# Fifteen small loads between the fifth K load and the fourth V load of a decode kernel

## The chip, the cores and the metric

The kernel runs on one core of one Trainium2 chip. The metric is device time in microseconds (us), the median of the runs shown. A profile is one execution of the same program recorded by the hardware profiler.

## What is computed

For eight sequences with one new position each, the kernel mixes an attention branch and an MLP branch by a gate. The attention has 32 query heads on 16 K/V heads of size 128 and looks at the last W = 2048 of 8192 cached positions. The model width is 576, the MLP width 4608. The inputs and the output are bf16.

```
W = 2048; rep = 2
q = (x @ wq).reshape(B, Sq, 32, 128).transpose(0, 2, 1, 3)
k = repeat(k_cache[:, :, -W:, :], rep, axis=1); v likewise
p = softmax(einsum("bhqd,bhkd->bhqk", q, k) * 128 ** -0.5)
a = einsum("bhqk,bhkd->bhqd", p, v) -> (B, Sq, 4096) @ wo
h = gelu(layernorm(x) @ w1 + b1)
b = h @ w2 + b2
g = sigmoid((x * gate_w).sum(-1))
out = g * a + (1 - g) * b
```

## The kernel before, in words

Nearly all the bytes are the K and V caches. They are read in sixteen units each (NU = 16, four groups of two sequences by four pieces of 512 positions). A unit of K or of V is one load of 4 MiB to all 128 partitions, 32 KB to each. The units share four slots of a large buffer in SBUF, `RAW` (`take_slot`, L606 to L609); a fifth area behind them holds the first part of wo. `load_item` (L613 to L621) takes the next slot and issues the load on SP's queue (L618), which waits until the slot's last readers are through: the transposes of a K unit on DVE (L718) or the P·V products of a V unit on PE (L755 and the loop around L188).

A K unit is transposed on DVE, multiplied with the query on PE (L732, and L175 for the products that keep their weights), its maximum is taken on DVE (L645), the exponential on ACT (L649), and the probabilities are transposed and spread (L668, L674). A V unit is then multiplied with them, and per group the four pieces are weighed together (`group_weights`, L691). The query projection (wq), the layernorm and w1 of the MLP come first; w2 and wo are the last loads, whose products add into one bank of PSUM (`AccGroup`, L570 on; its matmuls are L579). The two halves of the result are copied out on DVE and ACT (L900, L901) and stored by one DMA (L903), behind which SP waits once more (L904).

All loads are issued by SP, in the order of the program, through one queue: each `dma` names the one before it in `after=last_dma[-1:]`. At the start these are wq in two loads (L407, L408), four small ones, namely x with 8 rows of 1,152 bytes (L410), the gate with 1 row (L411), b1 with 4 rows of 2,304 bytes (L412) and b2 with 1 row of 1,152 bytes (L413), then w1 in two loads (L416, L417). After that the list `stream` (L587 to L594) sets the order: K0, K1, V0, K2, V1, K3, V2, K4, V3, K5 and so on, and at the end the parts of w2 and wo.

A DMA's semaphore grows by 16 when it has landed. The load of a slot counts on that slot's own semaphore; the keys stand in `dma_keys` (L376). All buffers lie in one arena, in the order of the `req` calls (L240 to L277), each aligned to 64 bytes and RAW to 512.

The order on each engine is made by a planner at build time (`_Plan.schedule`, L62 on), with a cost for each operation. It picks the operation that can start first by these costs. A DMA takes 0.35 us of its issuing engine (L43, L97). A load of less than 65536 bytes lands after the loads that are under way and a latency, and does not itself take time of the planner's one DMA channel (L98, L99); a larger one moves `dma_free` by its bytes (L101 to L103).

Of the kernel before, what the change touches and what calls it, by code (L numbers as in the profile page):

```python
# [6 lines left out]
BF = mybir.dt.bfloat16  # L7
# [31 lines left out]
class _Plan:  # L39
# [10 lines left out]
    def add(self, eng, fn, deps=(), name=None, cost=0.1, after=(), prio=0):  # L50
        op = _Op(eng, fn, deps, name, cost, after=after, prio=prio)
        op.idx = len(self.all)
        self.all.append(op)
        return op

    def dma(self, eng, fn, semkey, nbytes, deps=(), name=None, after=(), prio=0):
        op = _Op(eng, fn, deps, name, self.DMA_ISSUE, after=after, is_dma=True, dma_sem=semkey, nbytes=nbytes, prio=prio)
        op.idx = len(self.all)
        self.all.append(op)
        return op  # L60
# [134 lines left out]
def build_kernel(nc, A_x, A_k_cache, A_v_cache, A_wq, A_wo, B_x, B_w1, B_b1, B_w2, B_b2, gate_w, out):  # L195
    B, Sq, D = A_x.shape
# [3 lines left out]
    W = min(4096, max(256, Sk // 4))  # L200
# [8 lines left out]
    ND = 4  # L209
# [13 lines left out]
    out2 = out.rearrange("b s d -> (b s) d")  # L223

    with ExitStack() as es:
        R = {}
        aoff = [0]

        def req(name, nelem, dt, align=64):
            sz = 2 if dt == BF else 4  # L230
            o = aoff[0] + ARENA_BASE
            o = (o + align - 1) // align * align - ARENA_BASE
            R[name] = (o, nelem, dt)
            aoff[0] = o + nelem * sz
# [35 lines left out]
        req("X", 128, F32)  # L270
        req("XS", 2 * 128, BF)
        req("oT", WOP * 8, BF)
        req("BD", NK * 64, BF)
        req("P", 2048, BF)
        req("PC", 2048, BF)
# [30 lines left out]
        def view(name, parts=128):  # L306
            o, n, dt = R[name]
            a = arena[0:parts, o // 2: o // 2 + (n * (2 if dt == BF else 4)) // 2]
            if dt == F32:
                a = a.bitcast(F32)  # L310
            return a
# [31 lines left out]
        out_sb = view("out_sb")  # L343
# [18 lines left out]
        def col(i, parts=128):  # L362
# [10 lines left out]
        OC = 64  # L373

        eng_sems = {e: es.enter_context(nc.semaphore("sem_" + e)) for e in ENGS}
        dma_keys = ["x", "g", "b", "b2", "wq", "w1", "out"] + ["s%d" % i for i in range(ND + 1)] + ["t%d" % i for i in range(5)]  # L376
        dma_sems = {k: es.enter_context(nc.semaphore("dma_" + k)) for k in dma_keys}

        P = _Plan()
        add, dma = P.add, P.dma  # L380
# [7 lines left out]
                   deps=[o_idf], name="r8", cost=0.2)  # L388
# [198 lines left out]
        stream, nk = [], 0  # L587
# [8 lines left out]
        last_dma = [d_w1r]  # L596
# [26 lines left out]
        def query(g):  # L623
            qb_done[g] = []
            for a in range(4):
                def fn(e, a=a):
                    dst = bass.AP(arena, offset=32 * a * AST + aoffs("qbd") + 640 * (g % 2) + 32 * a + 16, ap=[[AST, 32], [160, 4], [1, 16]])
                    src = bass.AP(arena, offset=32 * a * AST + aoffs("q4") + 32 * (NB_ * g + a // 2) + 16 * (a % 2), ap=[[AST, 32], [256, 4], [1, 16]])
                    return e.tensor_copy(dst, src)  # L629
                qb_done[g].append(add("pool", fn, deps=o_q4 + [o_qz, qk_unit.get(NT * (g - 1) - 1)], name="qr%d_%d" % (g, a), cost=0.3))  # L630
# [224 lines left out]
        def bias(i):  # L855
            o_bias.append(AccGroup("m2_b", [(ob[:, 0:8], b2_sb), (ob[:, 8:16], b2_sb)], [d_b2, o_obl, o_obh], cost=0.6, after=[o_hp]).op)
# [17 lines left out]

        query(0)
        bias(0)
        for kind, i in stream:
            {"K": k_item, "V": v_item, "W": wo_chunk, "M": m2_chunk, "B": bias}[kind](i)

        seq = []  # L880
        for t in range(NU):
# [13 lines left out]
        fin = []  # L895
        for j, ev in enumerate(("dve", "act")):
# [3 lines left out]
                    return e.tensor_copy(dst, src)  # L900
                return e.activation(out=dst, in_=src, func=ACTF.Copy)  # L901
            fin.append(add(ev, ev_fn, deps=acc_ops, name="fin%d" % j, cost=0.4, prio=9))
        fin = [dma("sp", lambda e: e.dma_start(out2, out_sb[0:8, :]), "out", 8 * D * 2, deps=fin, name="d_out", after=last_dma[-1:])]  # L903
        add("sp", lambda e: e.sem_inc(eng_sems["sp"], 1), deps=fin, name="final_wait", cost=0.05)  # L904

        P.schedule()
# [6 lines left out]
def bass_gated_mix__sliding_block_cached__mixer_channel_mlp__decode_kernel(  # L913
    nc: bass.Bass,
    A_x: bass.AP,
    A_k_cache: bass.AP,
    A_v_cache: bass.AP,
    A_wq: bass.AP,
    A_wo: bass.AP,
    B_x: bass.AP,  # L920
    B_w1: bass.AP,
    B_b1: bass.AP,
    B_w2: bass.AP,
    B_b2: bass.AP,
    gate_w: bass.AP,
    out: bass.AP,
):
    build_kernel(nc, A_x, A_k_cache, A_v_cache, A_wq, A_wo, B_x, B_w1, B_b1, B_w2, B_b2, gate_w, out)
# [28 lines left out]
```

## Time and profile before

| what | value |
|---|---|
| median of 3 runs | 364.61 us (364.4 to 364.72) |
| span of the profiled execution, first to last instruction | 363.0 us |
| median less that span | 1.6 us |
| PE, DVE, ACT busy | 82%, 64%, 46% of the span |
| mean load rate | 426 GB/s, 154.45 MB in all |
| granted clock of PE, mean | 0.958 |

The time of the profiled execution outside its span is not given by itself; what lies around the span is taken as the difference in the third row.

The page gives, for each engine, its busy time and share of the span, and then the span in 40 slices of about 9.1 us with a digit for the busy tenth. "DMA" is the mean busy share of sixteen DMA engines. The load queue is q1 on the page; q8 and q14 fetch instructions through the same sixteen engines. A packet is one piece that one DMA engine moves: 32 KB for a row of a K or V load, 4 bytes for the write of a semaphore. The chain of waits goes back from the last instruction to what released each step. In a table of windows each row has a stretch of time, its length, the busy time of PE, PEld (weight loads), DVE, ACT and POOL in it with instruction counts, the granted clock, the DMA share and the rate of the loads; the last two count each packet wholly in the window in which it starts, so that in a very short window they can exceed what sixteen engines can do.

### The profile page before, as it was taken

To read this page: it belongs to the slowest core of one execution; us is meant where nothing else is said; L and a number is where in the kernel's file an instruction comes from. 1 tells how busy PE (TensorE), PEld (TensorE's weight loads), DVE (VectorE), ACT (ScalarE), POOL (GpSimd) and SP (SyncE) were. 2 spreads that over 40 slices of the span, in tenths; PEclk is the share of its full clock that TensorE was granted. 3 is DMA by queue.
4 is the path that set the end of the run, shared out by engine and by line. 5 is a ranking of instruction groups with operands and counts; after the bars stand their busy time and mean duration, and the time that the engine had idled before them with its cause. 6 is when DMAs were issued, how large, how long until landed. Compare 5 with 4: busy or idle time off the path is not lost.

```text
span 363.0 us, 4821 instructions
## 1 busy us (share of the span) xinstructions
PE 297.9 (82%) x1954; PEld 125.3 (35%) x1423; DVE 231.4 (64%) x166; ACT 168.6 (46%) x130; POOL 22.9 (6%) x52
## 2 busy tenths in 40 slices
PE   0456366999999979998897979997989698999875
PEld 0111000434252615242433417150615152436742
DVE  0452989576666694929385768566675949295720
ACT  1022106656647463663637373838374554656000
POOL 9032030000010000000100000000000000003000
PEclk9976598999999998999999989999999999999999
DMA  8999999999999999999999999999999999999996
GB/s 347 436 437 406 455 412 455 412 455 412 450 415 451 415 451 413 441 426 441 426 441 426 435 430 437 430 437 428 437 430 437 430 435 430 437 430 433 415 430 257
DMA packets 6102, 154.45 MB, mean 426 GB/s; under 512 B 694, under 2 KB 840, under 8 KB 1228
## 3 DMA queue, kind: packets, MB, share of 16 engines
q1 hardware_dynamic: 6092, 154.30, 98.8%
q8 instruction: 8, 0.13, 0.1%
q14 instruction: 2, 0.02, 0.0%
HBM read 154.29 MB, written 0.01 MB: 425 GB/s over the span
## 4 chain that ended last, share of the span: by engine, by line
DMA 56%; DVE 27%; PE 14%; issue 1%; ACT 1%; SPq 0%; POOL 0%
DMA arena<-in_A_k_cache_dram 47%; DVE arena L718 21%; PE ps L175 6%; DMA arena<-in_B_w_dram 6%; DMA arena<-in_A_x_dram 3%; DVE arena L668 2%; PE ps L188 2%; PE ps L755 2%; PE ps L732 2%; DVE arena L645 1%; PE ps L501 0%; PE ps L579 0%; DVE arena L557 0%; DVE arena L521 0%; ACT arena L536 0%
## 5 line engine op out<-in xcount | busy, mean ns | idle before, releaser
L718 DVE STREAM_TRANSPOSE arena<-arena 128x4096 f32<-128x4096 f32 (+1 forms) x34 | 141.7, 4175 | 21.9 <-DMA arena<-in_A_k_cache_dram 21.9
L674 ACT ACTIVATE arena<-arena 32x2048 bf16<-32x2048 bf16 x60 | 114.5, 1908 | 71.4 <-DVE arena L668 42.9
L175 PE MATMUL ps<-arena 128*128 128x512 bf16 (+3 forms) x531 | 136.1, 402 | 0.0
L188 PE MATMUL ps<-arena 128*128 x840 | 109.5, 277 | 7.3 <-issue 1.2
L188 PEld LDWEIGHTS ps<-arena 128*128 x840 | 81.4, 97 | 34.3 <-issue 19.0
L732 PE MATMUL ps<-arena 128*128 128x512 bf16 x128 | 51.4, 401 | 27.6 <-DVE arena L718 26.1
L645 DVE TENSOR_REDUCE arena<-ps 128x1 f32<-128x2048 f32 x16 | 36.7, 2291 | 53.8 <-PE ps L175 53.8
L732 PEld LDWEIGHTS ps<-arena 128*128 128x128 bf16 x128 | 12.5, 98 | 131.7 <-issue 75.3
L649 ACT ACTIVATE arena<-ps,arena 128x2048 bf16<-128x2048 f32 x16 | 40.7, 2543 | 0.5
L646 ACT ACTIVATE arena<-arena 128x1 f32<-128x1 f32 x16 | 3.2, 203 | 63.5 <-DVE arena L645 63.5
L755 PE MATMUL ps<-arena 128*128 128x256 bf16 x184 | 25.3, 272 | 1.1 <-DVE arena L663 1.1
L755 PEld LDWEIGHTS ps<-arena 128*128 128x128 bf16 x184 | 16.9, 99 | 18.8 <-issue 14.6
L668 DVE STREAM_TRANSPOSE arena<-arena 128x1024 f32<-128x1024 f32 x15 | 18.1, 1205 | 2.9 <-ACT arena L649 2.9
L579 PE MATMUL ps<-arena 128*8 128x288 bf16 (+1 forms) x140 | 9.6, 286 | 4.0 <-DMA arena<-in_A_wo_dram 3.3
L739 POOL MEMSET arena<- 128x4096 f32 x1 | 3.5, 3511 | 148.2 <-PE ps L175 148.2
L685 PE MATMUL ps<-arena 128*128 128x512 bf16 x16 | 6.5, 407 | 6.5 <-ACT arena L649 5.2
L629 POOL COPY arena<-arena 32x64 bf16<-32x64 bf16 x16 | 3.7, 229 | 123.3 <-PE ps L175 122.4
L901 ACT ACTIVATE arena<-ps 8x288 bf16<-8x288 f32 x1 | 0.4, 402 | 19.5 <-PE ps L579 19.5
L422 DVE COPY arena<-arena 8x128 bf16<-8x128 bf16 x2 | 0.5, 228 | 13.9 <-DMA arena<-in_A_x_dram 13.9
L579 PEld LDWEIGHTS ps<-arena 128*8 128x8 bf16 (+1 forms) x140 | 5.8, 86 | 9.9 <-DMA arena<-in_A_wo_dram 3.3
L900 DVE CAST arena<-ps 8x288 bf16<-8x288 f32 x1 | 0.4, 446 | 12.3 <-PE ps L579 12.3
L557 DVE TENSOR_TENSOR arena<-arena 128x1152 f32<-128x1152 f32 x1 | 1.4, 1358 | 9.7 <-ACT arena L555 9.7
(106 smaller groups left out, 94.0 us busy)
## 6 DMA issues: line engine op xcount, KB each, us to landing
arena<-in_A_k_cache_dram SPq DMA_DIRECT2D x16, 4096.0 KB, 28.7
arena<-in_A_v_cache_dram SPq DMA_DIRECT2D x16, 4096.0 KB, 25.5
arena<-in_B_w_dram SPq DMA_DIRECT2D x1, 4608.0 KB, 22.0
arena<-in_A_wo_dram SPq DMA_DIRECT2D x2, 2304.0 KB, 23.8
arena<-in_A_wq_dram SPq DMA_DIRECT2D x1, 4096.0 KB, 12.6
arena<-in_B_w_dram SPq DMA_DIRECT2D x1, 3456.0 KB, 24.1
arena<-in_B_w_dram SPq DMA_DIRECT2D x1, 1152.0 KB, 22.3
arena<-in_B_w_dram SPq DMA_DIRECT2D x1, 576.0 KB, 23.0
```

The lines of the kernel that those rows point to most:

```text
L175: return e.add_instruction(mybir.InstMatmult(name=nc.get_next_instruction_name(), engine=mybir.EngineType.PE, ins=[e.lower_ap(rhs), e.lowe ...
L188: return e.add_instruction(mybir.InstMatmult(name=nc.get_next_instruction_name(), engine=mybir.EngineType.PE, ins=[rhs, lhsT], outs=[e.low ...
L579: ins = e.matmul(ps[32 * j:32 * j + 8, BK_ACC, 0:JN], lhsT, rhs[:, JN * j:JN * j + JN], start=False, stop=True, skip_group_check=True, til ...
L629: return e.tensor_copy(dst, src)
L645: mx = add("dve", lambda e: e.tensor_reduce(out=k(g, MX + x), in_=scores, axis=AXL.X, op=ALU.max), deps=[qk_unit[t]], name="mx%d" % t, cos ...
L649: ex = add("act", lambda e: e.activation(out=bass.AP(arena, offset=aoffs("P"), ap=[[AST, 128], [64, 32], [1, 2], [2, 32]]), in_=ps[:, 0:4, ...
L668: pc = add("dve", lambda e: e.transpose(view("PC").bitcast(F32), view("P").bitcast(F32)), deps=[ex] + (sp_done[t - 1][0] if t else [o_acc0 ...
L674: return e.activation(out=bass.AP(arena, offset=32 * a * AST + aoffs(home) + 64 * a, ap=[[AST, 32], [256, 32], [1, 64]]), in_=bass.AP(aren ...
L685: mm = e.matmul(*args, start=True, stop=False, skip_group_check=True) if n == 0 else held_matmul(nc, e, *args, start=True, stop=False, ski ...
L718: return e.transpose(bass.AP(arena_f, offset=foffs(base) + 2048 * h0, ap=[[AST // 2, 128], [1, 2048 * nh]]), bass.AP(arena_f, offset=foffs ...
L732: mm = e.matmul(*args, start=False, stop=True, skip_group_check=True) if rc == 0 else held_matmul(nc, e, *args, stop=True, skip=True)
L755: return e.matmul(dst, bass.AP(arena, offset=aoffs(home) + 256 * q + ee, ap=[[AST, 128], [2, 128]]), slot(s).rearrange("p (r k d) -> p r k ...
```

## The change

Behind the eighth entry of `stream`, which is K4 (the fifth K), an entry `("R", 0)` is put in ahead of V3 (the fourth V). It issues fifteen loads on SP's queue, in the same chain `last_dma`. The n-th load, n = 1 to 15, reads the first 16 n elements of `B_b2` as n rows of 16 elements (32 bytes), and writes them to n partitions of a new buffer `probe`, each load to columns of its own. Nothing reads this buffer. The fifteen loads share one new semaphore, and the last instruction of SP waits for the last of them too. The output is computed as before.

```diff
         req("oT", WOP * 8, BF)
+        req("probe", 15 * 16, BF)
         req("BD", NK * 64, BF)
...
-        dma_keys = ["x", "g", "b", "b2", "wq", "w1", "out"] + ...
+        dma_keys = ["probe", "x", "g", "b", "b2", "wq", "w1", "out"] + ...
...
         query(0)
         bias(0)
+        probe = view("probe")
+        d_probe = []
+
+        def probes(i):
+            for n in range(1, 16):
+                d = dma("sp", lambda e, n=n: e.dma_start(probe[0:n, 16 * n - 16:16 * n], B_b2[0:16 * n].rearrange("(p c) -> p c", c=16)), "probe", 32 * n, name="d_probe%d" % n, after=last_dma[-1:])
+                last_dma.append(d)
+                d_probe.append(d)
+
+        stream.insert(8, ("R", 0))
         for kind, i in stream:
-            {"K": k_item, "V": v_item, "W": wo_chunk, "M": m2_chunk, "B": bias}[kind](i)
+            {"K": k_item, "V": v_item, "W": wo_chunk, "M": m2_chunk, "B": bias, "R": probes}[kind](i)
...
-        fin = [dma("sp", ..., name="d_out", after=last_dma[-1:])]
+        fin = [dma("sp", ..., name="d_out", after=last_dma[-1:])] + d_probe[-1:]
         add("sp", lambda e: e.sem_inc(eng_sems["sp"], 1), deps=fin, name="final_wait", cost=0.05)
```

More of the change, by code (lines that the diff above doesn't have):

```diff
@@ L375, in build_kernel @@
         eng_sems = {e: es.enter_context(nc.semaphore("sem_" + e)) for e in ENGS}
-        dma_keys = ["x", "g", "b", "b2", "wq", "w1", "out"] + ["s%d" % i for i in range(ND + 1)] + ["t%d" % i for i in range(5)]
+        dma_keys = ["probe", "x", "g", "b", "b2", "wq", "w1", "out"] + ["s%d" % i for i in range(ND + 1)] + ["t%d" % i for i in range(5)]
         dma_sems = {k: es.enter_context(nc.semaphore("dma_" + k)) for k in dma_keys}
@@ L902, in build_kernel @@
             fin.append(add(ev, ev_fn, deps=acc_ops, name="fin%d" % j, cost=0.4, prio=9))
-        fin = [dma("sp", lambda e: e.dma_start(out2, out_sb[0:8, :]), "out", 8 * D * 2, deps=fin, name="d_out", after=last_dma[-1:])]
+        fin = [dma("sp", lambda e: e.dma_start(out2, out_sb[0:8, :]), "out", 8 * D * 2, deps=fin, name="d_out", after=last_dma[-1:])] + d_probe[-1:]
         add("sp", lambda e: e.sem_inc(eng_sems["sp"], 1), deps=fin, name="final_wait", cost=0.05)
```

## The prediction

> **What bounds the kernel now.** I read the page first, then the chain of waits, then the issues of the load queue, and last the load traffic in narrow windows.
>
> ```profile
> span 363.0 us, 4821 instructions
> DMA  8999999999999999999999999999999999999996
> DMA packets 6102, 154.45 MB, mean 426 GB/s; under 512 B 694, under 2 KB 840, under 8 KB 1228
> q1 hardware_dynamic: 6092, 154.30, 98.8%
> q8 instruction: 8, 0.13, 0.1%
> ```
>
> The sixteen DMA engines are busy 98.8% of the span, from the second slice to the one before the last. No compute engine on this page comes near that: the kernel is a stream of loads, and the end moves when the stream gets longer. The chain of waits (start, length, what) says the same around the place of the change:
>
> ```profile
> 75.31 4.34 DVE arena L718
> 79.64 0.02 issue
> 79.66 25.41 DMA arena<-in_A_k_cache_dram
> 105.07 0.02 issue
> ...
> 115.15 28.60 DMA arena<-in_A_k_cache_dram
> ```
>
> The load issued at 79.66 us is the fifth K. It lands 25.41 us later although 4 MiB at 426 GB/s take 9.8 us, so some two and a half loads are ahead of it when it is issued. A load that is issued late by less than that backlog costs nothing. What costs is work that the DMA engines themselves do, or time in which one of them waits.
>
> **What the change puts on SP.** The queue's own timeline (start, duration):
>
> ```profile
> 1.71 0.37 SPq L410 DMA_DIRECT2D arena<-in_A_x_dram  x1
> 2.13 0.23 SPq L411 DMA_DIRECT2D arena<-in_gate_w_dram  x1
> 2.40 0.42 SPq L412 DMA_DIRECT2D arena<-in_B_b_dram  x1
> 2.87 0.33 SPq L413 DMA_DIRECT2D arena<-in_B_b_dram  x1
> ...
> 79.66 0.54 SPq L618 DMA_DIRECT2D arena<-in_A_k_cache_dram  x1
> 93.78 0.53 SPq L618 DMA_DIRECT2D arena<-in_A_v_cache_dram  x1
> ```
>
> The four small loads of the start took 0.23 to 0.42 us each to issue, from start to start about 0.4 us. Fifteen more are 15 x 0.4 = 6 us of SP. They follow the fifth K's issue, which is over at 80.20 us. The next issue, the fourth V's, comes at 93.78 us, since it waits for its slot. So 13.6 us of waiting lie there, 6 of them get filled, and nothing else is on SP. Cost **zero**. Without this cover the 6 us would still be hidden behind the backlog above.
>
> The planner charges 0.35 us per issue (L43), 5.25 us in all, less than that wait, and a load under 65536 bytes on SP does not move its `dma_free` (L98, L99). I therefore take the order of the other engines as unchanged. The new buffer has 480 bytes per partition; with the alignment to 64 every buffer behind it moves by 512 bytes, and RAW keeps its alignment to 512: zero. The final wait gets one more semaphore, reached 250 us before: one SP instruction behind the output's landing, under 0.1 us.
>
> **What it puts on the DMA engines.** From the packet counts one can read how a small load is spread. Under 512 bytes there are 694 packets. The 42 loads with 128 partitions (32 of K and V, two each of wq, w1 and wo, four of w2) give 42 x 16 = 672 if every engine that takes part writes one semaphore packet. That leaves 22, which is 8 + 8 for the 8-row input and output, 4 for the 4-row bias, and 1 + 1 for the two one-row loads. So a load to n rows runs on n engines, with one data packet and one semaphore packet on each. The fifteen loads add 1 + 2 + ... + 15 = 120 data packets of 32 bytes and as many semaphore packets. If the n engines are always the first n, engine 0 gets all fifteen loads, engine 1 fourteen, and so on down to engine 14 with one.
>
> The Trainium skill, "DMA: Bandwidth & Descriptors", section "Why a DMA increments its semaphore by 16 and not by 1", says that a DMA from SP uses the largest number of engines up to 16 that divides the outer sizes of both sides, and the lowest-numbered ones. The counts above agree with the number of engines; that they are the lowest-numbered ones no row of this page shows.
>
> What does one small load cost on an engine? The trace has one place with several behind each other: x, gate, b1 and b2, between wq and w1. In these windows the share counts a packet wholly where it starts, and GB/s times length gives its bytes:
>
> ```profile
> 13.44:13.45 0.01, 0.00 (x0) 0.00 (x0) 0.00 (x0) 0.00 (x0) 0.00 (x0) 1.00 0.62 231
> 13.45:13.57 0.12, 0.00 (x0) 0.00 (x0) 0.00 (x0) 0.00 (x0) 0.00 (x0) 1.00 2.22 922
> 13.57:13.74 0.17, 0.00 (x0) 0.00 (x0) 0.00 (x0) 0.00 (x0) 0.00 (x0) 1.00 0.00 0
> 13.74:13.80 0.06, 0.00 (x0) 0.00 (x0) 0.00 (x0) 0.00 (x0) 0.00 (x0) 1.00 0.06 19
> 13.80:13.84 0.04, 0.00 (x0) 0.00 (x0) 0.00 (x0) 0.00 (x0) 0.00 (x0) 1.00 0.00 0
> 13.84:13.87 0.03, 0.00 (x0) 0.00 (x0) 0.00 (x0) 0.00 (x0) 0.00 (x0) 1.00 3.23 1229
> ```
>
> A packet of w1 has 4 x 4608 x 2 = 36,864 bytes. In the first window start 231 GB/s x 0.01 us = 2.3 KB: one row of b1 (2,304 bytes), alone, with 0.62 x 16 x 0.01 us = 0.10 us of busy time. In the second 111 KB: three first packets of w1, on other engines. Then nothing starts for 0.17 us. At 13.74 to 13.80 come 19 GB/s x 0.06 us = 1.1 KB: this is b2's single row, with 0.06 x 16 x 0.06 us = 0.058 us of busy time, semaphore packet included. At 13.84 comes the sixteenth engine's first packet of w1 (36.9 KB). So one engine, the one with all the small loads, was **waiting, not working**: its b1 row starts near 13.45, its b2 row near 13.75, its first w1 packet at 13.85. That is 0.30 us and 0.10 us from start to start for loads that are busy for about 0.1 and 0.06 us.
>
> The price of one of the new loads on an engine therefore lies between two ends. Low end: no waiting, at most the 0.058 us of b2's row. High end: the 0.30 us from b1 to b2. I take the mean of the two steps, **0.20 us**, because back-to-back small loads on one engine are just what those rows show, and what they show is mostly waiting, which a row of 32 bytes instead of 1,152 does not shorten. Engine 0 then needs 15 x 0.20 = 3.0 us more.
>
> The skill's same page, section "Anatomy of one DMA — SWDGE (gpsimd) path", says "The trn2 sem-write bubble is tiny (~1 cycle)". By that sentence engine 0 would pay only busy time, and the sum would be 364.6 instead of 366.7; the gap of 0.17 us above speaks against it for small loads in a row, though not for large ones.
>
> **What hides part of it.** Every engine moves the same share of every load, without a pause, so a lag on one engine stays until the end, and the last engine sets each landing. Is engine 0 the last? Each of these windows holds one packet (its bytes are GB/s times length, 32.8 KB up to 105 us, 27.7 KB in the last two):
>
> ```profile
> 26.30:26.35 0.05, 0.05 (x2) 0.00 (x0) 0.00 (x0) 0.00 (x0) 0.05 (x1) 0.50 1.53 655
> 35.99:36.02 0.03, 0.00 (x0) 0.00 (x0) 0.03 (x1) 0.00 (x0) 0.00 (x0) 1.00 2.55 1092
> 36.90:36.93 0.03, 0.00 (x0) 0.00 (x0) 0.03 (x1) 0.00 (x0) 0.00 (x0) 0.50 2.55 1092
> 103.76:103.78 0.02, 0.02 (x3) 0.02 (x1) 0.02 (x1) 0.00 (x0) 0.00 (x0) 1.00 3.82 1639
> 104.67:104.69 0.02, 0.02 (x2) 0.00 (x0) 0.00 (x0) 0.02 (x1) 0.00 (x0) 1.00 3.82 1639
> 336.11:336.13 0.02, 0.02 (x3) 0.02 (x1) 0.02 (x1) 0.00 (x0) 0.00 (x0) 1.00 3.23 1383
> 337.13:337.15 0.02, 0.00 (x0) 0.00 (x0) 0.02 (x1) 0.00 (x0) 0.00 (x0) 1.00 3.23 1383
> ```
>
> The engine that started w1 last, at 13.85, starts its first K packet last of all, at 26.32, and the second K 9.68 us later, at 36.00. Seven loads of 9.68 us after that are 103.77: the same engine at the start of the fourth V. But by 36.92 another engine is later: an instruction packet (q8 on the page, eight of 16 KB) had taken time on it, and it stays behind, 104.68 at the same place. So engine 0 has **104.68 - 103.77 = 0.91 us** of slack where the small loads come, and 337.14 - 336.12 = 1.02 us near the end. I take 0.95 us.
>
> The end follows the last engine's landing:
>
> ```profile
> 360.79 0.09 PEld L579 LDWEIGHTS ps<-arena 128*8 128x8 bf16 x2 [0.15 <-DMA arena<-in_B_w_dram]
> 361.12 0.40 ACT L901 ACTIVATE arena<-ps 8x288 bf16<-8x288 f32 x1 [19.48 <-PE ps L579]
> 361.61 0.32 SPq L903 DMA_DIRECT2D out_dram<-arena  x1
> ```
>
> PE's last products wait for the last piece of w2, and the output's store follows, so a later landing moves the end one for one.
>
> **The sum.** SP 0, planner 0, layout 0, DMA engine 0: 3.0 - 0.95 = +2.05 us. If a low-numbered engine is among those that an instruction packet had put behind, its share is not covered: at most 14 x 0.20 = +2.8 us for engine 1. The trace does not name engines, so this stays in the range. The span of 363.0 us would become 365.05, and since the median of 364.61 us lies 1.6 us above that span, the time becomes 364.61 + 2.05 = **366.7 us**.
>
> **The rivals.**
>
> *No waiting, all hidden (not slower).* If a load costs engine 0 no more than the 0.058 us of b2's row, fifteen are 0.87 us, less than the 0.91 of slack, and the time stays at 364.6. It decides at 0.95 / 15 = 0.063 us per load. For it speak the large loads, whose semaphore packets leave no gap in the 98.8%; and the gap of 0.17 us is a single place. Against it: that place is the only one where small loads follow each other. Chance 0.28.
>
> *Waiting, mean 0.20 us per load.* As above; with the ends 0.10 (b2 to w1) and 0.30 (b1 to b2), engine 0 needs 1.5 to 4.5 us, the time becomes 364.61 + 0.55 to 364.61 + 3.55, and with engine 1 uncovered at the most 364.61 + 14 x 0.30 = 368.8. Chance 0.60.
>
> *Every small load waits for the one before it to land.* The nearest row is the output's store, the only small transfer that stands alone:
>
> ```profile
> SPq L904 <- DMA out_dram<-arena: 1.0, 1, 1.0
> ```
>
> At 1.0 us each, 15 us less 0.95 give 378.7. Against it: b1 to b2 took 0.30, not 1.0. What could bring it is a write of 32 bytes, which no load of this trace makes. The skill's page names 512 bytes as the limit below which a DMA engine reads, changes and writes back (section "Specifications"); no run here shows that. Chance 0.05.
>
> *The queue holds the issue back.* At the start ten loads were issued one behind the other, the last nine of them ahead of any long landing. Now up to eighteen would stand in the queue. If SP had to wait until the fifteen are through, near 105 us, the fourth V would be issued 11 us late and the stream would break for the time from an issue to data:
>
> ```profile
> arena<-in_A_wq_dram SPq DMA_DIRECT2D x1, 512.0 KB, 3.3
> ```
>
> The first load took 3.3 us to land, of which its bytes at 426 GB/s are 1.2, so 2.1 us: 366.7 alone, 368.8 with the waits. Nothing in the trace shows such a limit. Chance 0.04.
>
> *Faster.* The engine that is last could be spared an instruction packet if these fall on other engines; the next engine is about 0.1 us ahead of it, so at most 0.1 us is to be had. Chance 0.03 for anything beyond 0.2%.
>
> **How the numbers follow.** This measurement tells 0.2%, 0.73 us, from no change. The likeliest is the waiting case, 366.7 us. It falls below 365.34 only with less than 0.11 us per load, near its low end: I move 0.02 of its 0.60 to "within". So: slower 0.58 + 0.05 + 0.04 = 0.67, within 0.28 + 0.02 = 0.30, faster 0.03. The range from **364.5 to 368.8** takes in no change and the waiting case with both ends, and leaves out the landing case.
>
> **What would show it.** Right: 934 packets under 512 bytes (694 + 240), fifteen more issues between 80.2 and 87 us with the fourth V's still near 93.8, one engine's first packet of the fourth V some 3 us later than 103.77, a landing of it about 2 us later, and everything after that shifted by the same amount. Wrong: the first packet near 104.1 (no waiting), issues that stretch to 100 us (a full queue), or an order of instructions on PE or DVE that differs. A sum that is off with engine 0 as late as said would mean that the slack, or the engine that is last, was misread.

## The result and the profile after

The changed kernel takes **366.75 us** (366.04 to 367.54, 3 runs) against 364.61 us: a ratio of 1.0061, 95% interval 1.0045 to 1.0077, or +2.1 us. The profiled execution took 366.75 us, its span is 365.2 us, so 1.55 us lie around it, as before.

From the page of the changed kernel:

```profile
span 365.2 us, 4817 instructions
DMA packets 6342, 154.46 MB, mean 423 GB/s; under 512 B 934, under 2 KB 1080, under 8 KB 1468
q1 hardware_dynamic: 6332, 154.31, 98.3%
q8 instruction: 8, 0.13, 0.1%
```

Packets under 512 bytes went from 694 to 934, which is the 240 that were forecast, while the load queue's busy share fell from 98.8% to 98.3%. So the 2 us are not time in which the engines moved more; they stood still for longer. SP's queue around the change (start, duration):

```profile
79.99 0.54 SPq L619 DMA_DIRECT2D arena<-in_A_k_cache_dram  x1
80.57 5.40 SPq L883 DMA_DIRECT2D arena<-in_B_b_dram  x15
94.11 0.54 SPq L619 DMA_DIRECT2D arena<-in_A_v_cache_dram  x1
```

All fifteen are issued by 85.97, and the fourth V is issued 14.12 us after the fifth K, as before (93.78 - 79.66). By line, the weight loads of PE and the instructions of DVE, ACT and POOL come in the same order in both traces. What changed shows in short windows of the load traffic of the changed kernel (columns as in the prediction; the last two are DMA share and GB/s):

```profile
106.64:106.69 0.05, 0.01 (x1) 0.00 (x0) 0.05 (x1) 0.05 (x1) 0.00 (x0) 1.00 0.04 1
106.69:106.71 0.02, 0.00 (x0) 0.00 (x0) 0.02 (x1) 0.02 (x1) 0.00 (x0) 1.00 4.51 1638
106.93:106.95 0.02, 0.02 (x2) 0.02 (x1) 0.02 (x1) 0.02 (x1) 0.00 (x0) 1.00 3.82 1639
```

```profile
116.60:116.62 0.02, 0.02 (x1) 0.00 (x0) 0.00 (x0) 0.02 (x1) 0.00 (x0) 1.00 3.85 1639
116.62:116.64 0.02, 0.02 (x1) 0.00 (x0) 0.00 (x0) 0.02 (x1) 0.00 (x0) 1.00 3.79 1638
```

At 106.64 small packets alone are still starting (1 GB/s). The last two engines start the fourth V with one packet of 32.8 KB each near 106.70 and 106.94, some 3 us behind the 103.77 that the prediction took as a base, and the load behind it, the sixth K, near 116.61 and 116.62. The packet of 106.94 takes 3.82 x 16 x 0.02 = 1.22 us, as an ordinary one does, so on this engine the wait stands among the small loads, as forecast. Before, the last two did that here:

```profile
114.33:114.35 0.02, 0.02 (x2) 0.00 (x0) 0.02 (x1) 0.02 (x1) 0.00 (x0) 1.00 3.79 1638
114.35:114.36 0.01, 0.01 (x2) 0.00 (x0) 0.01 (x1) 0.01 (x1) 0.00 (x0) 1.00 0.00 0
114.36:114.38 0.02, 0.02 (x2) 0.00 (x0) 0.02 (x1) 0.02 (x1) 0.00 (x0) 1.00 3.82 1639
```

So the last engine is 116.62 - 114.37 = 2.25 us later, one load after the change, and this stays to the end. The timeline of the end of the changed kernel:

```profile
362.60 0.44 PEld L580 LDWEIGHTS ps<-arena 128*8 128x8 bf16 x8 [0.24 <-DMA arena<-in_B_w_dram]
363.30 0.40 ACT L912 ACTIVATE arena<-ps 8x288 bf16<-8x288 f32 x1 [19.50 <-PE ps L580]
363.79 0.32 SPq L914 DMA_DIRECT2D out_dram<-arena  x1
```

The output's store is issued at 363.79 instead of 361.61: 2.18 us later.

### The profile page after: what moved, and what is told of

The parts are those of the page before. It is cut to its first block, busy times and chain, and to the rows that moved or that the text cites. A ratio compares the mean times of both kernels' runs of the same rounds, so it can differ in the third digit from the quotient of the medians.

```text
span 365.2 us, 4817 instructions
## 1 busy us (share of the span) xinstructions
PE 295.9 (81%) x1935; PEld 125.1 (34%) x1423; DVE 231.5 (63%) x166; ACT 168.7 (46%) x130; POOL 23.0 (6%) x52
## 3 DMA queue, kind: packets, MB, share of 16 engines
q1 hardware_dynamic: 6332, 154.31, 98.3%
## 4 chain that ended last, share of the span: by engine, by line
DMA 62%; DVE 24%; PE 12%; SPq 1%; issue 1%
DMA arena<-in_A_k_cache_dram 56%; DVE arena L719 20%; DMA arena<-in_B_w_dram 6%; PE ps L175 5%; DVE arena L669 2%; PE ps L188 2%; PE ps L756 2%; PE ps L733 2%; DVE arena L646 1%; PE ps L580 0%; DVE arena L911 0%; SPq L418 0%; SPq L409 0%; SPq L408 0%; SPq L411 0%
## 5 line engine op out<-in xcount | busy, mean ns | idle before, releaser
L733 PE MATMUL ps<-arena 128*128 128x512 bf16 x122 | 49.1, 402 | 20.6 <-DVE arena L719 18.9
L686 PE MATMUL ps<-arena 128*128 128x512 bf16 x11 | 4.4, 399 | 5.2 <-ACT arena L650 5.2
L795 DVE SCALAR_TENSOR_TENSOR arena<-ps,arena 128x256 f32<-128x256 f32 x12 | 5.7, 476 | 2.8 <-PE ps L756 2.7
```

What stands on the lines that cost most here:

```text
L686: mm = e.matmul(*args, start=True, stop=False, skip_group_check=True) if n == 0 else held_matmul(nc, e, *args, start=True, stop=False, ski ...
L733: mm = e.matmul(*args, start=False, stop=True, skip_group_check=True) if rc == 0 else held_matmul(nc, e, *args, stop=True, skip=True)
L795: fn = lambda e, src=src, w=w: e.scalar_tensor_tensor(out=X2, in0=src, scalar=w, in1=X2, op0=ALU.mult, op1=ALU.add)
```

## The experiments

The theory of the prediction: the most loaded engine pays about 0.20 us for each small load that stands behind another, less the slack that it had. Its rivals: the number of packets counts, not the engine; a packet of 32 bytes is slow in itself; SP is what costs. Each group of experiments ran on one chip beside the kernel before, and each difference is to the median of those runs. The edits are to the changed kernel, mostly to its loop, and the small loads' data are read by nothing, so no part of the computation is touched.

### One row each

```diff
-  dma("sp", ... probe[0:n, 16 * n - 16:16 * n], B_b2[0:16 * n].rearrange("(p c) -> p c", c=16)) ...
+  dma("sp", ... probe[0:1, 16 * n - 16:16 * n], B_b2[0:16].rearrange("(p c) -> p c", c=16)) ...
```

> All fifteen loads go to one row, so only one DMA engine gets any, and it still gets all fifteen: 15 data packets of 32 bytes instead of 120. Theory (the busiest engine counts: it waits about 0.2 us per load when small loads stand behind each other, less the 0.95 us by which another engine was already later): as with the change, 2.1 us over the kernel before, about 366.7. Rival A (the packets of all engines take a share of something common, so their number counts): an eighth of the cost, about +0.3 us.

Measured: 365.16 us against 364.53, +0.6 us, ratio 1.0013 (1.0004 to 1.0022). The theory missed by a factor of three. The windows of this run show where engine 0's time went:

```profile
103.54:103.72 0.18, 0.18 (x4) 0.15 (x2) 0.18 (x1) 0.00 (x0) 0.00 (x0) 1.00 0.09 3
103.72:103.74 0.02, 0.02 (x2) 0.02 (x1) 0.02 (x1) 0.00 (x0) 0.00 (x0) 1.00 7.52 1638
103.74:104.00 0.26, 0.26 (x4) 0.21 (x3) 0.26 (x1) 0.00 (x0) 0.00 (x0) 1.00 0.00 0
115.16:115.19 0.03, 0.03 (x2) 0.00 (x0) 0.03 (x1) 0.03 (x1) 0.00 (x0) 1.00 2.55 1092
```

In the first row all fifteen small loads start within 0.18 us, without a gap: 0.09 x 16 x 0.18 = 0.26 us of busy time, 0.017 us each. The second row is one packet of 32.8 KB, the first of the fourth V on this engine, and it is busy for 7.52 x 16 x 0.02 = 2.41 us; an ordinary one is 3.82 x 16 x 0.02 = 1.22 us. So the wait does not stand between the small loads here, it stands **in the big packets behind them**: the second one takes 1.79 us, and from the third on they are ordinary. Engine 0 starts the load after that at 115.17. A big load takes an engine 9.68 us, so fifteen loads cost it 115.17 - 103.54 - 9.68 = 1.95 us, 0.13 us each. The end moved by only 0.6 us; the rest was covered by the slack.

The trace's semaphore events of these loads, which come when a packet's semaphore write lands, point to what takes the time (us):

```
104.045 104.230 104.414 104.599 104.784 104.968 105.153 ... 106.488 106.673
```

Fifteen writes from one engine land (106.673 - 104.045) / 14 = 0.188 us apart, long after the packets were started at 0.012 us intervals. The second big packet ends at 107.909, which is 1.24 us after the last of these landings. This gives a new theory, W: an engine's semaphore writes go one after the other, and the write side of the next big packets waits behind them; some of that is hidden, because the engine reads ahead meanwhile. That the engine reads ahead is part of the theory; no run shows it.

### Sixteen rows each

```diff
+  dma("sp", ... probe[0:16, 16 * n - 16:16 * n], B_b2[0:256].rearrange("(p c) -> p c", c=16)) ...
```

> Every one of the fifteen loads goes to 16 rows, so each of the sixteen engines gets all fifteen, the last one too. Theory: the slack of 0.95 us no longer covers anything, +3.0 to +3.4 us over before, about 368. Rival A (the number of packets counts, 240 instead of 120): twice the cost of the change, +4.3 us. Rival S (what costs is SP, which issues as many loads as in the change): +2.1 us.

Measured: 367.63 us, +3.1 us, 1.0082 (1.0068 to 1.0095). The theory's forecast is met here, though it missed with one row. Rival S falls: SP issues fifteen loads here and with one row, and the costs are 3.1 and 0.6 us. Rival A falls too as a count: twice the packets of the change cost 1.5 times as much, and an eighth of them 0.3 times.

### One small load at a time

```diff
-  for n in range(1, 16):
+  for n in [i]:
...
-  stream.insert(8, ("R", 0))
+  for n in range(15, 0, -1):
+      stream.insert(8 + n - 1, ("R", n))
```

> The same fifteen loads to n rows, but one ahead of each of the fifteen big loads from the fourth V on, so that never two small ones follow each other. Theory (the waiting comes from small loads in a row; one alone finds its descriptors ready): engine 0 pays 15 x 0.02 us of busy time, inside its slack, so +0.0 to +0.2 us. Rival P (each small load has its price wherever it stands): +2.1 us as with the change.

Measured: 364.65 us, +0.1 us, 1.0000 (0.9991 to 1.0009). Rival P falls. The same packets cost nothing that can be measured when no two small loads stand together.

### One load with as many pieces

```diff
-  for n in range(1, 16):
-      d = dma("sp", ...)
+  for n in [1]:
+      d = dma("sp", lambda e, n=n: e.dma_start(probe[0:16, :].rearrange("p (c w) -> p c w", w=16), B_w1[0:16, 0:15 * 128].rearrange("p (c w) -> p c w", w=128)[:, :, 0:16]), "probe", 32 * 240, ...)
```

> One load in place of the fifteen, which gives each of sixteen engines 15 pieces of 32 bytes from separate places of w1 and one semaphore packet. Theory (the waiting is per load, not per packet): 15 x 0.01 us on each engine, +0.1 to +0.3 us. Rival W (a write or read of 32 bytes is what takes long): 15 pieces on every engine, none with slack, +3 us.

Measured: 364.73 us, +0.2 us, 1.0003 (0.9994 to 1.0012). With 16 rows and fifteen loads the same 240 pieces of 32 bytes cost 3.1 us. What differs is 240 semaphore packets against 16, and fifteen loads against one (and the source, of which more below). Rival W of that expectation, slow pieces of 32 bytes, falls.

### Thirty loads to one row

```diff
-  req("probe", 15 * 16, BF)
+  req("probe", 30 * 16, BF)
...
-  for n in range(1, 16):
+  for n in range(1, 31):
...
+  dma("sp", ... probe[0:1, 16 * n - 16:16 * n], B_b2[0:16].rearrange("(p c) -> p c", c=16)) ...
```

> Thirty loads to one row instead of fifteen; only engine 0 gets them. With fifteen it was about 1.9 us late, of which its slack took all but 0.6. Theory W (the semaphore writes of one engine go one after the other, 0.187 us apart, and all but about 0.9 us of that holds the engine up): 30 x 0.187 - 0.9 = 4.7 us on engine 0, less 1.1 of slack, +3.6 us. Rival L (a fixed net price of 1.9 / 15 = 0.13 us each): 3.9 - 1.1 = +2.7 us. The price of the prediction, 0.20 us each: 6.0 - 0.95 = +5.0 us.

Measured: 368.82 us against 364.45, +4.4 us, 1.0122 (1.0107 to 1.0138). The windows of this run:

```profile
103.41:103.68 0.27, 0.27 (x3) 0.03 (x1) 0.27 (x1) 0.00 (x0) 0.14 (x1) 1.00 0.10 3
...
104.04:104.06 0.02, 0.02 (x2) 0.02 (x1) 0.02 (x1) 0.00 (x0) 0.00 (x0) 1.00 14.75 1639
```

```profile
117.80:117.82 0.02, 0.02 (x2) 0.00 (x0) 0.00 (x0) 0.02 (x1) 0.00 (x0) 1.00 3.79 1638
```

The first big packet behind thirty small loads is busy for 14.75 x 16 x 0.02 = 4.72 us. Engine 0 lost 117.81 - 103.41 - 9.68 = 4.72 us in all, as W had it (4.7), and 2.77 us more than with fifteen: **0.185 us for each further load**, the spacing of the semaphore writes. The second big packet again ends 1.24 us after the last landing (110.545 - 109.309). The end moved by 4.4 us, more than the 3.6 of W. Some 0.9 us of it lie behind the loads:

```profile
364.45 0.40 ACT L912 ACTIVATE arena<-ps 8x288 bf16<-8x288 f32 x1 [19.46 <-PE ps L580]
365.34 0.32 SPq L914 DMA_DIRECT2D out_dram<-arena  x1
```

The copies of the output start 364.45 - 361.12 = 3.33 us later than before, so the slack covered 1.4 us of the 4.72. The store is issued 0.89 us after that instead of 0.49, and SP waits 1.5 us for it instead of 1.0. Why the store took longer in this run is open.

### A longer row, on other partitions

```diff
-  req("probe", 15 * 16, BF)
+  req("probe", 512, BF)
...
+  dma("sp", ... probe[8 * n:8 * n + 1, 0:512], B_b2[0:512].rearrange("(p c) -> p c", c=512)) ...
```

> Fifteen loads to one row as in the first experiment (+0.6 us), but of 1,024 bytes instead of 32, each to another partition. Rival R (writes under 512 bytes are slow): the waits go, busy time of 15 x 0.047 = 0.7 us stays inside the slack, 0.0 us. Rival T (the partition decides which engine moves a row): the loads fall on different engines, 0.0 us. Theory W: the writes wait as before, and the 15 x 0.037 us of the longer rows lie beside that or add to it: +0.6 to +1.3 us.

Measured: 365.26 us against 364.59, +0.7 us, 1.0019 (1.0010 to 1.0028): what 32 bytes cost. Rival R falls, since rows of 1,024 bytes are no cheaper. Rival T falls, since fifteen different partitions did not spread the loads over engines. The semaphore events are 0.184 to 0.192 us apart here too.

### Eight rows each, and a semaphore for each load

```diff
+  dma("sp", ... probe[0:8, 16 * n - 16:16 * n], B_b2[0:128].rearrange("(p c) -> p c", c=16)) ...
```

> All fifteen loads go to 8 rows, so engines 0 to 7 get fifteen each and 8 to 15 none; as many data packets (120) as in the change. Theory I (engines do not disturb each other, the count on an engine decides): engine 0 as with one row, and the end +0.6, or up to +1.9 if an engine that an instruction packet had put behind is among the first eight. Rival D (engines with small loads disturb each other): +2 to +3 us, between one row and 16 rows or like the latter.

Measured: 366.87 us against 364.45, +2.4 us, 1.0073 (1.0059 to 1.0086). Theory I falls, since it allowed at most +1.9: with eight engines at it the end moves further than one engine's own waits explain. The second kernel of this pair left the loads as in the change:

```diff
-  dma_keys = ["probe", ...
+  dma_keys = ["probe%d" % n for n in range(1, 16)] + [...
...
-  fin = [dma("sp", ..., name="d_out", ...)] + d_probe[-1:]
+  fin = d_probe + [dma("sp", ..., name="d_out", ...)]
```

> The change, but each of the fifteen loads counts on a semaphore of its own. If the writes of all engines to one semaphore get in each other's way, the cost falls towards that of one engine alone, +0.6 us. If the order of the writes within each engine is what counts, or the data, nothing changes: +2.1 us.

Measured: 366.58 us, +2.1 us, 1.0062 (1.0048 to 1.0076), the same as the change. Engines do disturb each other, but not because they write to one semaphore.

With a semaphore for each load, the trace also tells the landings of the loads apart (us):

```
load 1:  103.939
load 2:  103.811 104.126
load 3:  103.721 103.990 104.309
load 4:  103.897 104.171 104.491 104.717
...
load 15: 103.836 103.861 ... 106.136 106.526 106.975
```

The n-th load has n landings, and they join into fifteen series, of fifteen, fourteen and so on down to one, with steps of 0.16 to 0.22 us and one of 0.41: the staircase of the prediction. The series with fifteen runs from 103.939 to 106.526, a step of 0.185 us, as for one engine alone. But it is not the last. The latest series begins only with the fourth load, at 104.717, and ends at 106.975: an engine with **twelve** loads. After the row the last engine starts the sixth K at 116.26 and the next one at 115.01. The one at 115.01 has its second big packet end at 107.753, 1.23 us after 106.526, so by the distance found above it is the engine with fifteen, and the end in this run is set by the engine with twelve.

### Another source

```diff
-  B_b2[0:16 * n].rearrange("(p c) -> p c", c=16)
+  B_w1[32 * n:33 * n, 128 * n:128 * n + 16]
```

> The change with another source: the n-th load reads its n rows of 32 bytes from n different rows of w1 (9,216 bytes apart) and another place for each n, instead of all from the first 480 bytes of b2. Rival M (what slows the loads of several engines is that all read the same few bytes of memory): the cost falls to +0.6 us or less. Theory W (the ordered semaphore writes): unchanged, +2.1 to +2.4 us.

Measured: 365.67 us against 364.59, +1.1 us, 1.0031 (1.0018 to 1.0043). Neither expectation holds by itself: **half of the change's 2.1 us came with the source**, one place of 480 bytes that many engines read fifteen times, and half is left. Both M and W are part of the cause. The edit moves the rows apart and gives each load its own rows at once, so whether it is the same bytes or only bytes close together that delay the engines is not told apart. With this source every small packet starts right behind the one before, as with one row, and the windows show single engines:

```profile
103.60:103.77 0.17, 0.17 (x4) 0.12 (x2) 0.17 (x1) 0.00 (x0) 0.00 (x0) 1.00 0.10 3
103.77:103.79 0.02, 0.02 (x2) 0.02 (x1) 0.02 (x1) 0.00 (x0) 0.00 (x0) 1.00 7.82 1639
103.79:103.92 0.13, 0.13 (x3) 0.11 (x2) 0.13 (x1) 0.00 (x0) 0.00 (x0) 1.00 0.00 0
103.92:104.06 0.14, 0.14 (x3) 0.12 (x2) 0.14 (x1) 0.00 (x0) 0.00 (x0) 1.00 0.10 3
104.06:104.08 0.02, 0.02 (x2) 0.01 (x1) 0.02 (x1) 0.00 (x0) 0.00 (x0) 1.00 6.48 1638
```

The first row is 0.10 x 16 x 0.17 = 0.27 us of small packets, fifteen loads at 0.018, then a big packet of 7.82 x 16 x 0.02 = 2.50 us: this is the engine with all fifteen. The fourth row is 0.22 us, twelve loads, then a big packet of 6.48 x 16 x 0.02 = 2.07 us: another engine, with the loads n = 4 to 15, the fourth in the staircase. So the n-th load does go to the same first n engines each time. In this kernel, too, the engine with fifteen starts the sixth K near 115.32, so it lost 115.32 - 103.60 - 9.68 = 2.04 us, hardly more than alone (1.95), and its second big packet ends 1.24 us after its last landing here too (108.055 - 106.817). With the rows apart, the other engines hardly disturb it.

### Five at a time

```diff
-  for n in range(1, 16):
+  for n in range(5 * i + 1, 5 * i + 6):
...
+  dma("sp", ... probe[0:16, 16 * n - 16:16 * n], B_b2[0:256].rearrange("(p c) -> p c", c=16)) ...
...
-  stream.insert(8, ("R", 0))
+  for i in range(2, -1, -1):
+      stream.insert(8 + 4 * i, ("R", i))
```

> The fifteen loads to 16 rows, which cost 3.1 us in one row of fifteen, but in three groups of five, ahead of the fourth, sixth and eighth V. Theory W (semaphore writes 0.19 to 0.25 us apart, the first 0.9 us of each row hidden because the big packet behind is read ahead meanwhile): 5 x 0.19 to 0.25 is 0.95 to 1.25, less 0.9, three times: +0.2 to +1.0 us. Rival L (a price per load): +3.1 us.

Measured: 365.85 us against 364.59, +1.3 us, 1.0037 (1.0023 to 1.0051), a little over W's end, far from 3.1. And with the source changed in this kernel:

```diff
-  B_b2[0:256].rearrange("(p c) -> p c", c=16)
+  B_w1[32 * n:32 * n + 16, 128 * n:128 * n + 16]
```

> The three groups of five loads to 16 rows, but each row read from another row of w1 (9,216 bytes apart) instead of all from the first 512 bytes of b2. With the shared source the three groups cost 1.26 us. Theory W (semaphore writes of an engine 0.187 us apart, the first 0.9 us of each row hidden behind the reading ahead of the big packet): 5 x 0.187 is 0.94, so 0.0 to 0.1 us a group, +0.0 to +0.3 us in all. If the source does not matter: +1.3 us. If nothing is hidden: 3 x 0.94 = +2.8 us.

Measured: 365.23 us against 364.40, +0.8 us, 1.0023 (1.0012 to 1.0033). The source matters here as well. But W forecast 0.3 at the most: a group of five still costs 0.28 us, so the hidden part is less than the 0.9 us that one engine alone has. "The first 0.9 us is free" does not hold as a fixed amount.

### Issued by ACT

```diff
-  d = dma("sp", ..., after=last_dma[-1:])
-  last_dma.append(d)
+  d = dma("act", ..., after=last_dma[-1:])
```

> The same fifteen loads to n rows, issued by ACT on its own queue while the fifth K is under way, instead of standing in SP's queue. Theory Q (what waits is the order within one queue; the big loads of SP's queue go on past it): +0.0 to +0.3 us over before. Rival E (each engine itself is held by the writes behind a small load, whichever queue it came from): about +2.1 us, as with the change.

Measured: 365.26 us against 364.45, +0.8 us, 1.0022 (1.0013 to 1.0031), between the two. It does not tell them apart. The row of the new line shows why:

```profile
L883 ACTq DMA_DIRECT2D arena<-in_B_b_dram x15: 248/317/519, 76.7 to 104.7; - x15
```

ACT issued the loads between its own instructions over 28 us, so they no longer stood in a row, and the order of the queue and the row were changed at once.

## Why the prediction was right, and which step of it was not

**SP, planner and layout at zero: right.** The issues took 5.40 us, less than the 6 reckoned, inside the wait for the slot; the other engines' order is the same; the one-row runs issue as many loads and cost a third.

**The spreading: right.** 240 more packets, and the fifteen series of landings, of fifteen down to one, in the run with a semaphore for each load show the same engines each time. The Trainium skill's rule that was cited there ("DMA: Bandwidth & Descriptors", section "Why a DMA increments its semaphore by 16 and not by 1"), the lowest-numbered engines, agrees with that as far as the trace can show it, since the trace names no engine. Fifteen partitions 8 apart did not change it.

**The price of 0.20 us on engine 0: the step that failed.** It was read from the one place with small loads in a row, as a wait between packets of one engine, and was taken to hold for an engine by itself. Alone, engine 0 pays 1.95 us for fifteen, 0.13 each, and 0.185 for each load beyond; and the wait then shows in the big packets behind. The change's larger cost has a second part that the prediction did not have: the loads of many engines read one place of 480 bytes. With rows apart the change costs 1.1 us, not 2.1. The choice of engine 0 as the one that counts failed with it, at least in the run with a semaphore for each load, which costs what the change costs: an engine with twelve loads is 1.26 us behind the one with fifteen there (116.262 - 115.005). The prediction had the case that a low-numbered engine's share is not covered, but only in its range.

**The slack: there, but taken too small.** With one row, engine 0 is 1.95 us late and the end 0.6 us, so 1.3 us was covered, and with thirty loads 1.4, where 0.95 was taken. Part of this is that engine 0 came to the row at 103.54 and 103.41 in those two runs, not at 103.77. Where all engines get fifteen loads nothing is covered and the cost is 3.1 us.

**The sum.** +2.05 us was forecast and +2.1 measured. By its own terms the prediction would have given +2.05 us for the run with one row as well, and that measured +0.6. So the agreement of the total is partly luck: a price that was too high for one engine, less a slack that was too small, stood in for what the engines do to each other.

**The rivals.** "No waiting" is refuted by the changed kernel. The Trainium skill's sentence behind it, a semaphore write of "~1 cycle" (same page, section "Anatomy of one DMA — SWDGE (gpsimd) path"), stands in a section on loads that gpsimd issues, while those here are issued by SP. It agrees with loads that stand alone (+0.1 us for fifteen) and not with rows of them: 0.188 us from landing to landing. Waiting for each landing (+14 us) and writes below 512 bytes as the cause did not come, the latter refuted by rows of 1,024 bytes. A full queue did not come.

**What stays open.** That the order of the semaphore writes is the cause is argued from their spacing, the equal marginal price, the fixed 1.24 us from the last landing to the end of the second big packet, and the one load with 240 pieces (from another source); loads without a semaphore write would show it, and no run here has them. Another cost that each load brings once, in step with these writes, is not excluded. Why reading one place delays the engines, and how much of a short row is hidden, stays open. So does which engine was last in the changed kernel itself: its last two start the sixth K within 0.02 us of each other, and with one semaphore their landings can't be told apart.

## What to carry to other kernels

In a stream of loads that is the bound, a small load standing alone between big ones costs nothing that shows, but a row of them costs an engine that takes part in it: 0.13 us per load for fifteen here, 0.185 for each load beyond, and more where many engines read one place. The time can appear in the big packets behind. Put the pieces into one load (+0.2 us, where fifteen loads of as many pieces cost +3.1, though from one shared place) or put them one at a time between big loads (+0.1 us instead of +2.1), and be wary of many engines reading the same few bytes. In these runs a load to few rows fell on few engines, the same ones each time, so see first whether these have slack against the engine that lands last.

## What the runs showed of the hardware that was not expected

- Semaphore writes of one DMA engine alone land 0.184 to 0.193 us apart, whether the row before them has 32 or 1,024 bytes, and on one semaphore or fifteen the change costs the same 2.1 us.
- Behind fifteen and thirty small loads one packet of 32 KB takes 2.41 and 4.72 us instead of 1.22, and the packet after it ends 1.24 us after the last semaphore write has landed.
- Reading one place of 480 bytes from up to fifteen engines, instead of rows 9,216 bytes apart, doubled the cost of the change, 2.1 against 1.1 us.
